# A residual block with two convolutions: image sums moved from TensorE to VectorE and ScalarE, warm-up matmuls, and the first tile's chain put ahead

## The chip, the cores and the metric

The kernel runs on one core of one Trainium2 chip, in one launch. The metric is the device time of that launch in microseconds, taken as the median of several executions. A shorter time is better.

The core has five engines that run their own instruction streams in order and wait for each other through semaphores: TensorE (PE, matrix products into the accumulator memory PSUM), VectorE (DVE), ScalarE (ACT), GpSimd (POOL) and SyncE (SP), which here issues the hardware DMAs. POOL issues the DMAs that add into their target.

## The reference, cut to what matters

Two images (B = 2) of 512 channels and 64x64 pixels go through group norm, SiLU and a 3x3 convolution, twice; an embedding is added between, and the input at the end.

```python
B, C, HW, E = 2, 512, 64, 1152
def reference(x, t_emb, g1, be1, w1, w_emb, g2, be2, w2):
    G, eps = 4, 1e-5
    def gn(z, gamma, beta):
        zr = z.reshape(B, G, (C // G) * H * W)
        mu = zr.mean(-1).reshape(B, G, 1)
        var = ((zr - mu) ** 2).mean(-1).reshape(B, G, 1)
        ...
        return zn * gamma.reshape(1, C, 1, 1) + beta.reshape(1, C, 1, 1)
    def conv3(z, w):
        taps = [jnp.einsum("bchw,oc->bohw", zp[:, :, i:i+H, j:j+W], w[:, :, i, j]) for i in range(3) for j in range(3)]
        ...
    h = conv3(_silu(gn(x, g1, be1)), w1)
    emb = _silu(t_emb) @ w_emb
    h = h + emb.reshape(B, C, 1, 1)
    h = conv3(_silu(gn(h, g2, be2)), w2)
    return x + h
```

A group of the norm is 128 channels, so it is one tile of 128 partitions: each tile needs the mean and the mean square of 128 x 4096 elements before its SiLU can start. All arrays are bf16.

## The kernel before, in words

**Tiles and chunks.** Channels are cut into four tiles `ct` of 128 partitions. The work is cut into eight chunks `c`: layer, image, half of the image's rows. Chunks 0 and 1 are image 1 in the first convolution, 2 and 3 image 2 in the first, 4 to 7 the same in the second. A chunk is four units `k`, one for each tile of output channels. The convolution is computed in a transformed form: six row points `s` = 0 to 5 (`rows_a`, `rows_b` make them on DVE out of the SiLU's output), and, from chunk 1 on, for some of the points a second transform along the columns. A unit is a sequence of matmul groups named by what they compute: `p` (three taps, moving operand of 512 columns), `B` and `A` (nested, 256 columns each). ACT copies each finished PSUM bank out (`evac_...`), DVE combines the points into the output rows.

**Order.** Nothing runs in the order in which it is written. `Plan.op` notes each operation with its engine, an estimated cost and the regions it reads and writes; `Plan.solve` schedules all of them by a list scheduler with priorities from the end backwards, and `emit` writes the instructions by their planned start. So each engine's queue is the planner's order. Main matmuls (`chain=True`) keep the order in which they were written; the others (statistics, norms, embedding) are put between them. Two numbers steer that: `slack`, a time in us by which the planner keeps such a PE operation after its inputs, and `boost`, which lets one be picked earlier.

**The opening.** For each of the four tiles of image 1 the first half (`XB0`, 34 rows of 65) and the second half (`XB1`, 32 rows) are loaded by SP, and `stats0(ct)` forms the sums:

- `ones(...)`: eight matmuls of 260 columns with a matrix of ones (`ones_bf`) for each half, which add over channels; one ACT instruction then sums the 260 columns (the mean);
- `gram(...)`: seventeen matmuls of the first half with itself (`128x128` and one `32x32`), whose diagonal a DVE instruction at L1081 takes out (mean square of the first half);
- an ACT `Square` with accumulation over 2080 elements for the mean square of the second half.

`gn_chain` then adds over partitions (small f32 matmuls with `ones_neg`), and through a few DVE instructions of one column and one power on POOL (L453) gives the scale and shift of the tile's SiLU (`silu`, ACT, 2112 elements). `rows_a` makes points 4 and 5 (one `TENSOR_SCALAR` of 2145 and three `TENSOR_TENSOR` of 1040 elements on DVE), and the 18 matmuls of these points for three output tiles follow ("o" below: 18 for each `ct`, 72 in all).

**Image 2.** `stats1(ct)` does the same for image 2, while chunk 0 computes: per tile four loads of 1040 columns into three rotating buffers, four `ones` matmuls and one ACT `Square` with accumulation for each piece, and one ACT sum of 260 columns at the end. That is 64 matmuls and 16 squares. Chunk 2 needs the result.

**Lines.** All planned matmuls stand at L381, ACT's at L353, DVE's two-operand ones at L330 and its scalings at L334, DMAs at L366.

Of the kernel before, what the change touches and what calls it, by code (L numbers as in the profile page):

```python
# [10 lines left out]
ACT = mybir.ActivationFunctionType  # L11
ALU = mybir.AluOpType
# [13 lines left out]
class Plan:  # L26
# [7 lines left out]
    def __init__(self):  # L34
        self.ops = []
        self.spaces = {}
        self.chain = None

    def _space(self, name, size):
        if name not in self.spaces:  # L40
# [6 lines left out]
    def op(self, eng, cost, fn, r=(), w=(), name="", chain=False, lat=None, slack=0.0, after=None, sw=False, boost=0.0):  # L47
        o = Op()
        o.i, o.eng, o.cost, o.fn, o.name = len(self.ops), eng, cost, fn, name
        o.lat = self.LAT[eng] if lat is None else lat  # L50
        o.slack = slack
        o.sw = sw
        o.boost = boost
        deps = set()
        for sp, idx in r:
            deps.update(np.unique(self.spaces[sp][0][idx]).tolist())
        for sp, idx in w:
            lw, rd, mask = self.spaces[sp]
# [119 lines left out]
def _idx(off, dims):  # L178
# [27 lines left out]
    's': ((A_, A_, A_), (D_, D_, D_), (D_, A_, A_), (D_, D_, D_), (A_, A_, A_), (A_, A_, D_), (A_, A_, A_), (D_, A_, D_)),  # L206
    'oacc': (1, 1),
    'np': 1,
    'pre': 13,
    'wpe': (1, 0, 0, 0),  # L210
    'vacc': (0, 1, 1, 1, 1, 1, 1, 0),
# [4 lines left out]
def kernel(  # L216
# [97 lines left out]
    def Fc(n):  # L314
        c = fcur[0]
        fcur[0] += n
        assert fcur[0] <= NF
        return c
# [4 lines left out]
    def T(ap, key):  # L323
        return R(ap, K(key), 1)
# [58 lines left out]


    make_identity(nc, ident[:])
    nc.vector.memset(ones_neg[:], -1.0 / P)
    nc.vector.memset(ones_bf[:], 1.0)
    cneg = T(ones_neg[:], "cneg")
    cone = T(ones_bf[:], "cone")
    cid = T(ident[:], "cid")  # L390
    gp, tp = T(gparm[:], "gparm"), T(tparm[:], "tparm")
    GB = Fc(4 * CT)
    EMB = Fc(CT * BB)
    SC = Fc(2 * BB * CT)
# [32 lines left out]
    def small(fn, r, w, name, cost=0.125):  # L427
        pl.op("DVE", cost, fn, regs(*r), regs(*w), name)

    def gn_chain(layer, b, ct, mes, name, SB=7, slack=2.5, n=1):  # L430

        V = nc.vector
        ps = Ps(SB, 0, [[1, 2 * n]])
# [612 lines left out]
    memz("gpsimd", A(AB[0], [[1, RW]]), "az")  # L1046
    memz("gpsimd", A(AB[1], [[1, RW]]), "az")

    def stats0(ct):
        nm = f"st0{ct}"  # L1050
        me = Fc(2)
        mg = Fc(1)
        bk = 6 + (ct % 2)
        jk = YS[1] + (ct % 2) * 1040
        G0 = 260
        b_ = psum[:]

        def ones(base, first):
            mm([(Ps(bk, 0, [[1, 260]]), cone, A(base + i * 260, [[1, 260]], BF16), first and i == 0, False)
                for i in range(8)], nm, chain=False, slack=0.0, warm=cold)  # L1060

        def gram(base, last):
            lst = []
            for i in range(17):
                n = 128 if i < 16 else 32
                blk = A(base + i * 128, [[1, n]], BF16)
                q_ = psum[0:n]
                lst.append((R(bass.AP(q_.tensor, q_.offset + bk * 512 + G0, [list(q_.ap[0]), [1, n]]),
                              ("P", np.array([bk])), n), blk, blk, False, i == 16))
            mm(lst, nm, chain=False, slack=0.0, warm=cold)  # L1070

        cold = 1.7 if ct == 0 else 1.0
        ones(XB0[ct] + RW, True)
        gram(XB0[ct] + RW, False)
        cold = 1.0
        ones(XB1[ct], False)
        x1 = A(XB1[ct], [[1, YF]], BF16)
        act(A8(jk, YF), x1, ACT.Square, scale=float(HW) ** -0.5, acc=F(me + 1), name=nm)
        g = Ps(bk, G0, [[1, 128]])
        j2 = A(MB + 1024 + (ct % 2) * 512, [[1, 128]], BF16)  # L1080
        pl.op("DVE", 0.3, lambda: nc.vector.scalar_tensor_tensor(  # L1081
            out=j2.ap, in0=g.ap, scalar=1.0 / HW, in1=ident[:], op0=ALU.mult, op1=ALU.mult, accum_out=F(mg).ap),
            regs(g), regs(j2, F(mg)), nm)
        junk = A(MB + (ct % 2) * 512, [[1, 260]], BF16)
        act(junk, Ps(bk, 0, [[1, 260]]), ACT.Identity, scale=1.0 / (P * HW), acc=F(me), name=nm)
        gn_chain(0, 0, ct, [(me, 0, 2), (mg, 1, 1)], nm, SB=bk, slack=0.0)

    IDS = {}
    for i, v in enumerate((-1.0, 2.0, -2.0, 4.0)):
# [6 lines left out]
    def pe_w1(ct):  # L1096

        nm = f"w1_0{ct}"
        d = A(RAW[ct % 2] + 1152, [[1, 384]], BF16)
        dma(d.ap, w1[0][:, 3072 + ct * 384:3072 + (ct + 1) * 384], [], [d], P * 768, nm)  # L1100
        load_ur_ct(0, ct)
        w0 = UREG[0] + 7168 + ct * 768
        lst = []
        for s, (c0, c2, c1) in enumerate(((1.0, 1.0, -1.0), (1.0, 4.0, -2.0), (1.0, 1.0, 1.0), (1.0, 4.0, 2.0))):
            for i, (cf, src) in enumerate(((c0, w0), (c2, w0 + 384), (c1, RAW[ct % 2] + 1152))):
                lst.append((Ps(s, 0, [[1, 384]]), IDS[cf], A(src, [[1, 384]], BF16), i == 0, i == 2))
        mm(lst, nm, chain=False, slack=0.0)
        act(A(UREG[0] + ct * 1792, [[128, 4], [512, 3], [1, 128]]), Ps(0, 0, [[512, 4], [128, 3], [1, 128]]), ACT.Copy, name=nm)

    for ct in range(CT):  # L1110
        if CFG["wpe"][ct]:
            pe_w1(ct)
    for ct in range(CT):
        d = A(XB0[ct], [[1, AF]], BF16)
        dma(d.ap, x[0, ct, 0], [], [d], P * AF * 2, f"x0{ct}", lat=3.1)
        d = A(XB1[ct], [[1, YF]], BF16)
# [4 lines left out]
        rows_a(0, ct, WB[ct % 3], CFG["k0"][ct], True)  # L1121
        for j in range(3):
# [13 lines left out]
    def stats1(ct):  # L1136
        nm = f"st1{ct}"
        me, mq = ME1 + ct, ME1 + CT + ct
        bk = 6 + ct % 2
        part = Fc(4)  # L1140
        for i in range(4):
# [4 lines left out]
            mm([(Ps(bk, 0, [[1, 260]]), cone, A(pb + 260 * q, [[1, 260]], BF16),  # L1146
                 i == 0 and q == 0, i == 3 and q == 3) for q in range(4)], nm, chain=False, boost=15.0)
            act(A8(VB[0] + 3 * VP + 3120 + i % 2 * 520, 1040), d, ACT.Square, scale=float(HW) ** -0.5, acc=F(part + i), name=nm)
        act(A(VB[0] + 3 * VP + 3120, [[1, 260]], BF16), Ps(bk, 0, [[1, 260]]), ACT.Identity, scale=1.0 / (P * HW), acc=F(me), name=nm)
        pl.op("DVE", 0.1, lambda: nc.vector.reduce_sum(out=F(mq).ap, in_=F(part, 4).ap, axis=AX.X),  # L1150
              regs(F(part, 4)), regs(F(mq)), nm)
        if ct == CT - 1:
            later.append(lambda: gn_chain(0, 1, 0, [(ME1, 0, 2 * CT)], "st1", n=CT))

    def emb():
        nm = "emb"
        at = [VB[0] + i // 2 * VP + 3120 + i % 2 * 512 for i in range(8)] + [JNK]
        for i in range(0, ET, 2):
# [143 lines left out]
```

## Time and profile before

| | |
|---|---|
| median of 5 runs | 468.43 us (466.42 to 469.41) |
| the profiled execution | 468.97 us |
| its span, first to last instruction | 467.2 us |
| PE, DVE, ACT busy | 452.0, 418.6, 373.1 us |
| POOL busy | 84.2 us |
| granted TensorE clock, mean | 0.998 |
| HBM read, written | 62.25, 31.32 MB |
| `ones` matmuls (128x260) | 128, busy 18.5 us |
| `gram` matmuls (128x128) | 64, busy 5.3 us |
| ACT `Square` of image 2 (128x1040) | 16, mean 1076 ns |

The profiled execution lasts 1.8 us longer than its span; it lies 0.5 us above the median. "Busy" of PE counts a matmul from its start to its modelled end, and the ends of one overlap the start of the next; the distance from one start to the next is the time that a matmul costs a full PE. ACT instructions with accumulation are followed by a short `ACTIVATION_READ_ACCUMULATOR`, most of which overlaps.

### The profile page before, as it was taken

How to read it: one execution, taken by the hardware profiler on the slowest of the kernel's cores; microseconds unless marked ns; L12 is line 12 of the kernel's file. 1: busy time of each engine (PE TensorE's matmuls, PEld its weight loads, DVE VectorE, ACT ScalarE, POOL GpSimd, SP SyncE). 2: the span in 40 equal slices, each digit the busy share in tenths (PEclk: the TensorE clock that was granted, in tenths of full speed). 3: DMA queues.
4: the chain of work that ended last, by engine and by line, in shares of the span. 5: the costliest groups of instructions: out<-in, count | busy, mean ns of one | idle time of the engine just before them, and what ended most of it. 6: DMA issues, size and time to landing. Idle time of an engine off the chain costs nothing.

```text
span 467.2 us, 8376 instructions
## 1 busy us (share of the span) xinstructions
PE 452.0 (97%) x2968; PEld 286.5 (61%) x2968; DVE 418.6 (90%) x807; ACT 373.1 (80%) x588; POOL 84.2 (18%) x110
## 2 busy tenths in 40 slices
PE   6989999999999999999999999999999999999994
PEld 5745554455555555455555576666677776678883
DVE  0599999998799999965998899989999799999997
ACT  5899999677989976889959869778776989567662
POOL 4010011121120121120211111232233211231210
PEclk9999999999999999999999999999999999999999
DMA  8974775499868589984898979867998696676834
GB/s 324 364 278 120 204 201 155 114 293 326 231 160 227 163 208 277 267 268 164 219 291 253 349 262 279 226 96 178 252 219 193 139 228 138 137 167 127 161 72 91
DMA packets 50138, 98.38 MB, mean 211 GB/s; under 512 B 7088, under 2 KB 22320, under 8 KB 50096
## 3 DMA queue, kind: packets, MB, share of 16 engines
q1 hardware_dynamic: 35520, 77.60, 48.6%
q0 software_dynamic: 14288, 20.24, 28.4%
q8 instruction: 23, 0.38, 0.3%
q14 instruction: 19, 0.16, 0.1%
q10 hardware_dynamic: 288, 0.01, 0.0%
HBM read 62.25 MB, written 31.32 MB: 200 GB/s over the span
## 4 chain that ended last, share of the span: by engine, by line
PE 46%; DVE 6%; DMA 3%; ACT 2%; issue 2%; DVEq 0%; SPq 0%; ACTq 0%
PE psum L381 46%; DVE ar L330 6%; ACT ar L353 2%; DMA ar<-u_scr 2%; DMA ar<-ar 1%; DVE ar L334 0%; DVEq L1297 0%; SPq L366 0%; DVE fs L1026 0%; DVE fs L1027 0%; DVEq L330 0%; DVE fs L1029 0%; DVE fs L1031 0%; DVE fs L1034 0%; DVE fs L1028 0%
## 5 line engine op out<-in xcount | busy, mean ns | idle before, releaser
L381 PE MATMUL psum<-ar 128*128 128x256 f16 (+2 forms) x2761 | 434.6, 319 | 1.5 <-DMA ar<-in_w_dram 1.4
L330 DVE TENSOR_TENSOR ar<-ar 128x1040 f16<-128x1040 f16 (+7 forms) x649 | 393.6, 665 | 28.9 <-ACT ar L353 19.9
L381 PEld LDWEIGHTS <-ar 128*128 128x128 f16 (+1 forms) x2797 | 269.7, 98 | 160.0 <-issue 2.2
L353 ACT ACTIVATE ar<-ar 128x384 bf16<-128x384 bf16 (+6 forms) x185 | 159.0, 898 | 46.2 <-DVE ar L330 22.8
L353 ACT ACTIVATE ar<-psum 128x512 f16<-128x512 f32 (+2 forms) x232 | 159.7, 715 | 29.2 <-PE psum L381 17.1
L366 POOL DMA_DIRECT2D ar<-ar x46 | 50.5, 1115 | 229.8 <-DVE ar L330 126.7
L353 ACT ACTIVATE ar<-ar,fs 128x2112 f16<-128x2112 bf16 (+1 forms) x32 | 68.9, 2157 | 7.0 <-DMA ar<-h_scr 2.6
L366 POOL DMA_DIRECT2D out_dram<-ar x15 | 18.5, 1234 | 48.8 <-DMA ar<-ar 30.2
L334 DVE TENSOR_SCALAR ar<-ar 128x512 f16<-128x512 f16 (+2 forms) x73 | 26.0, 383 | 1.0 <-ACT ar L353 1.0
L381 PE MATMUL psum<-ar,ones_bf 128*128 128x260 bf16 x128 | 18.5, 283 | 4.5 <-DMA ar<-in_x_dram 4.5
L353 ACT ACTIVATION_READ_ACCUMULATOR ar<-psum 128x1 f32 x100 | 21.7, 217 | 0.0
L381 PEld LDWEIGHTS <-ones_bf 128*128 128x128 bf16 x128 | 12.5, 101 | 9.6 <-issue 3.2
L370 POOL MEMSET ar<- 128x65 f16 (+6 forms) x30 | 6.4, 273 | 58.8 <-ACT ar L353 25.5
L453 POOL TENSOR_TENSOR fs<-fs 128x1 f32<-128x1 f32 (+1 forms) x7 | 7.2, 1025 | 32.3 <-DVE fs L451 32.3
L1081 DVE SCALAR_TENSOR_TENSOR ar<-psum,ident 128x128 bf16<-128x128 f32 x4 | 1.2, 289 | 8.3 <-PE psum L381 8.3
L353 ACT ACTIVATION_READ_ACCUMULATOR ar<-ar 128x1 f32 x36 | 7.6, 210 | 0.0
L381 PEld LDWEIGHTS psum<-fs,ones_neg 128*128 128x128 f32 x36 | 4.7, 191 | 3.5 <-ACT ar L353 3.3
L381 PE MATMUL psum<-fs,ones_neg 128*128 128x1 f32 (+3 forms) x36 | 4.6, 241 | 2.3 <-ACT ar L353 2.3
L444 DVE COPY fs<-psum 128x2 f32<-128x2 f32 (+1 forms) x7 | 1.1, 159 | 1.7 <-PE psum L381 1.7
L412 ACT ACT_TABLE_LOAD x1 | 1.3, 1283 | 1.7 <-PEq L1286 1.7
L416 DVE CAST fs<-gparm 128x16 f32<-128x16 bf16 x1 | 0.2, 174 | 2.6 <-DMA gparm<-in_params_dram 2.6
L417 ACT ACTIVATE s_sb<-tparm 128x18 bf16<-128x18 bf16 x1 | 0.2, 218 | 2.8 <-DMA tparm<-in_t_emb_dram 2.8
(40 smaller groups left out, 18.8 us busy)
## 6 DMA issues: line engine op xcount, KB each, us to landing
ar<-in_w_dram SPq DMA_DIRECT2D x32, 384.0 KB, 5.2
ar<-ar POOLq DMA_DIRECT2D x46, 260.0 KB, 4.9
ar<-in_x_dram SPq DMA_DIRECT2D x16, 552.5 KB, 4.5
h_scr<-ar SPq DMA_DIRECT2D x16, 520.0 KB, 5.1
ar<-h_scr SPq DMA_DIRECT2D x16, 520.0 KB, 4.6
out_dram<-in_x_dram SPq DMA_DIRECT2D x30, 260.0 KB, 5.2
out_dram<-ar POOLq DMA_DIRECT2D x15, 520.0 KB, 6.0
u_scr<-ar SPq DMA_DIRECT2D x16, 384.0 KB, 3.9
```

Source lines behind the costliest of these rows:

```text
L330: pl.op("DVE", 0.075 + 0.000521 * out.n, lambda: nc.vector.tensor_tensor(out=out.ap, in0=a.ap, in1=b.ap, op=op), regs(a, b), regs(out), name)
L334: pl.op("DVE", cost or 0.075 + 0.00026 * out.n, lambda: nc.vector.tensor_scalar(out=out.ap, in0=a.ap, scalar1=s, scalar2=None, op0=ALU.mul ...
L353: lambda: nc.scalar.activation(out=out.ap, in_=a.ap, func=func, scale=sc, **kw), regs(*rr), regs(*ww), name)
L366: lambda: eng.dma_start(out=out, in_=in_, **kw), regs(*r), regs(*w), name, lat=lat or (4.5 if sw else None), after=after, sw=sw)
L370: pl.op("POOL" if eng == "gpsimd" else "DVE", 0.08 + 0.0005 * out.n, lambda: e.memset(out.ap, v), (), regs(out), name)
L381: nc.tensor.matmul(out.ap, lhsT=lhsT.ap, rhs=rhs.ap, start=st, stop=sp, skip_group_check=True)
L412: nc.scalar.activation(out=fs[:, WARM:WARM + 1], in_=fs[:, WARM + 1:WARM + 2], func=ACT.Silu)
L416: nc.vector.tensor_copy(out=fs[:, GB:GB + 4 * CT], in_=gparm[:])
L417: nc.scalar.activation(out=s_sb[:], in_=tparm[:], func=ACT.Silu)
L444: pl.op("DVE", 0.16, lambda: V.tensor_copy(out=F(tot, 2 * n).ap, in_=ps.ap), regs(ps), regs(F(tot, 2 * n)), name, boost=bo)
L453: pl.op("POOL", 0.85 if n == 1 else 1.9, lambda: nc.gpsimd.tensor_tensor(out=F(rs, n).ap, in0=N.ap, in1=F(NEGH, n).ap, op=ALU.pow), regs(N ...
L1081: pl.op("DVE", 0.3, lambda: nc.vector.scalar_tensor_tensor(out=j2.ap, in0=g.ap, scalar=1.0 / HW, in1=ident[:], op0=ALU.mult, op1=ALU.mult, ...
```

## The change

1. **Image 1's sums** (`stats0`), by a table `'st0'` with a letter for each half of each tile: `D` is `bn_stats` on DVE (five pieces of 416 elements, then `bn_aggr` and two small instructions that turn mean and variance into mean and mean square); `A` is the `ones` matmuls with ACT's square; `P` is the `ones` matmuls with the gram. The table is `('DA', 'DA', 'DP', 'PP')`.
2. **Image 2's sums** (`stats1`): for each piece ACT runs a second pass, `Identity` with accumulation, in place of the four `ones` matmuls; a DVE `reduce_sum` adds the four partial sums.
3. **Warm-up**: nine matmuls of 512 columns on `ones_bf`, with no data to wait for, before all others.
4. **First tile ahead**: `push` adds to the boost of all operations of tile 0's chain (40, and 20 more for its first load).
5. **Smaller pieces**: `gram` is planned as two operations, the weights' `pe_w1` matmuls as four, the embedding's 36 as nine, the latter with `slack` 0 for 2.5.
6. **`slack` of `gn_chain`** by default 5.0 for 2.5, which concerns image 2's first norm and both norms of the second layer.

```diff
-        o.boost = boost
+        o.boost = boost + self.push
...
+    'st0': ('DA', 'DA', 'DP', 'PP'),
+    'st1': 'AAAA',
+    'warm': 9,
+    'push': (40.0, 0.0, 0.0, 0.0),
...
+    for i in range(CFG["warm"]):
+        nc.tensor.matmul(psum[:, 0:512], lhsT=ones_bf[:], rhs=wr, start=True, stop=True, skip_group_check=True)
...
-    def gn_chain(layer, b, ct, mes, name, SB=7, slack=2.5, n=1):
+    def gn_chain(layer, b, ct, mes, name, SB=7, slack=5.0, n=1):
...
+    def bn(pieces, out, scale, name):
+        mv = Fc(2)
+        V = nc.vector
+        for i, d in enumerate(pieces):
+            pl.op("DVE", 0.07 + 0.00104 * d.n, lambda d=d, i=i: V.bn_stats(out=F(BNS + 6 * i, 6).ap, in_=d.ap),
+                  regs(d), regs(F(BNS + 6 * i, 6)), name)
+        S_, M_, W_ = F(BNS, 6 * len(pieces)), F(mv), F(mv + 1)
+        small(lambda: V.bn_aggr(out=F(mv, 2).ap, in_=S_.ap), [S_], [F(mv, 2)], name, 0.15)
...
+        for h, base in enumerate((XB0[ct] + RW, XB1[ct])):
+            if how[h] == "D":
+                me = Fc(2)
+                bn([A(base + i * 416, [[1, 416]], BF16) for i in range(5)], F(me, 2), YF / HW, nm)
+                mes.append((me, 0, 2))
+                continue
+            ones(base, cold)
+            if how[h] == "P":
+                gram(base, cold, "P" not in how[h + 1:])
+            else:
+                sq = Fc(1)
+                act(A8(jk, YF), A(base, [[1, YF]], BF16), ACT.Square, scale=float(HW) ** -0.5, acc=F(sq), name=nm)
+                mes.append((sq, 1, 1))
...
-        mm(lst, nm, chain=False, slack=0.0)
+        for i in range(0, 12, 3):
+            mm(lst[i:i + 3], nm, chain=False, slack=0.0)
...
+        pl.push = CFG["push"][ct]
+        pl.push += 20.0 if ct == 0 else 0.0
...
+            if CFG["st1"][ct] == "A":
+                act(A8(VB[0] + 3 * VP + 3120 + i % 2 * 520, 1040), d, ACT.Identity, scale=1.0 / HW, acc=F(psum_ + i), name=nm)
...
-        mm(lst, nm, chain=False)
+        for i in range(0, len(lst), CT):
+            mm(lst[i:i + CT], nm, chain=False, slack=0.0)
```

Since the planner orders everything anew, the queues of all engines differ from before, also where the operations are the same.

More of the change, by code (lines that the diff above doesn't have):

```diff
@@ L37, in __init__ @@
         self.chain = None
+        self.push = 0.0
     def _space(self, name, size):
@@ L385 @@
     make_identity(nc, ident[:])
+    nc.vector.memset(ones_bf[:], 1.0)
     nc.vector.memset(ones_neg[:], -1.0 / P)
-    nc.vector.memset(ones_bf[:], 1.0)
     cneg = T(ones_neg[:], "cneg")
@@ L391 @@
     gp, tp = T(gparm[:], "gparm"), T(tparm[:], "tparm")
+    wr = ones_bf[:]
+    wr = bass.AP(wr.tensor, wr.offset, [list(wr.ap[0]), [0, 4], [1, P]])
+    for i in range(CFG["warm"]):
+        nc.tensor.matmul(psum[:, 0:512], lhsT=ones_bf[:], rhs=wr, start=True, stop=True, skip_group_check=True)
     GB = Fc(4 * CT)
@@ L1047 @@
     memz("gpsimd", A(AB[1], [[1, RW]]), "az")
+    BNS = Fc(96)
+    def bn(pieces, out, scale, name):
[6 more added lines that the diff above has]
+        small(lambda: V.bn_aggr(out=F(mv, 2).ap, in_=S_.ap), [S_], [F(mv, 2)], name, 0.15)
+        small(lambda: V.scalar_tensor_tensor(
+            out=W_.ap, in0=M_.ap, scalar=M_.ap, in1=W_.ap, op0=ALU.mult, op1=ALU.add), [M_, W_], [W_], name)
+        small(lambda: V.tensor_scalar(
+            out=out.ap, in0=F(mv, 2).ap, scalar1=scale, scalar2=None, op0=ALU.mult), [F(mv, 2)], [out], name)
     def stats0(ct):
         nm = f"st0{ct}"
-        me = Fc(2)
-        mg = Fc(1)
         bk = 6 + (ct % 2)
@@ L1055, in stats0, with ones, gram @@
         G0 = 260
-        b_ = psum[:]
-        def ones(base, first):
-            mm([(Ps(bk, 0, [[1, 260]]), cone, A(base + i * 260, [[1, 260]], BF16), first and i == 0, False)
+        how = CFG["st0"][ct]
+        begun = []
+        def ones(base, cold):
+            mm([(Ps(bk, 0, [[1, 260]]), cone, A(base + i * 260, [[1, 260]], BF16), not begun and i == 0, False)
                 for i in range(8)], nm, chain=False, slack=0.0, warm=cold)
-        def gram(base, last):
+            begun.append(0)
+        def gram(base, cold, last):
             lst = []
@@ L1068, in gram @@
                 lst.append((R(bass.AP(q_.tensor, q_.offset + bk * 512 + G0, [list(q_.ap[0]), [1, n]]),
[L1069 to L1086, printed above, removed]
+                              ("P", np.array([bk])), n), blk, blk, False, last and i == 16))
@@ new lines, in gram @@
+            mm(lst[:8], nm, chain=False, slack=0.0, warm=cold)
+            mm(lst[8:], nm, chain=False, slack=0.0, warm=cold)
+        mes = []
+        for h, base in enumerate((XB0[ct] + RW, XB1[ct])):
+            cold = 1.0
+            if how[h] == "D":
[10 more added lines that the diff above has]
+                mes.append((sq, 1, 1))
@@ new lines, in stats0 @@
+        if "P" in how:
+            mg = Fc(1)
+            g = Ps(bk, G0, [[1, 128]])
+            j2 = A(MB + 1024 + (ct % 2) * 512, [[1, 128]], BF16)
+            pl.op("DVE", 0.3, lambda: nc.vector.scalar_tensor_tensor(
+                out=j2.ap, in0=g.ap, scalar=1.0 / HW, in1=ident[:], op0=ALU.mult, op1=ALU.mult, accum_out=F(mg).ap),
+                regs(g), regs(j2, F(mg)), nm)
+            mes.append((mg, 1, 1))
+        if begun:
+            s1 = Fc(1)
+            junk = A(MB + (ct % 2) * 512, [[1, 260]], BF16)
+            act(junk, Ps(bk, 0, [[1, 260]]), ACT.Identity, scale=1.0 / (P * HW), acc=F(s1), name=nm)
+            mes.insert(0, (s1, 0, 1))
@@ L1088 @@
+        gn_chain(0, 0, ct, mes, nm, SB=bk, slack=0.0)
     IDS = {}
@@ L1113 @@
     for ct in range(CT):
+        pl.push = CFG["push"][ct]
+        pl.push += 20.0 if ct == 0 else 0.0
         d = A(XB0[ct], [[1, AF]], BF16)
         dma(d.ap, x[0, ct, 0], [], [d], P * AF * 2, f"x0{ct}", lat=3.1)
+        pl.push = CFG["push"][ct]
         d = A(XB1[ct], [[1, YF]], BF16)
@@ L1121 @@
         rows_a(0, ct, WB[ct % 3], CFG["k0"][ct], True)
+        pl.push = 0.0
         for j in range(3):
@@ L1138, in stats1 @@
         me, mq = ME1 + ct, ME1 + CT + ct
+        use_bn = CFG["st1"][ct] == "D"
         bk = 6 + ct % 2
         part = Fc(4)
+        psum_ = Fc(4)
+        pieces = []
         for i in range(4):
@@ L1145, in stats1 @@
             dma(d.ap, x[1, ct, i // 2][:, r0 * RW:(r0 + 16) * RW], [], [d], P * 2080, nm)
-            mm([(Ps(bk, 0, [[1, 260]]), cone, A(pb + 260 * q, [[1, 260]], BF16),
-                 i == 0 and q == 0, i == 3 and q == 3) for q in range(4)], nm, chain=False, boost=15.0)
-            act(A8(VB[0] + 3 * VP + 3120 + i % 2 * 520, 1040), d, ACT.Square, scale=float(HW) ** -0.5, acc=F(part + i), name=nm)
-        act(A(VB[0] + 3 * VP + 3120, [[1, 260]], BF16), Ps(bk, 0, [[1, 260]]), ACT.Identity, scale=1.0 / (P * HW), acc=F(me), name=nm)
-        pl.op("DVE", 0.1, lambda: nc.vector.reduce_sum(out=F(mq).ap, in_=F(part, 4).ap, axis=AX.X),
-              regs(F(part, 4)), regs(F(mq)), nm)
+            if use_bn:
+                pieces += [A(pb + 260 * q, [[1, 260]], BF16) for q in range(4)]
+                continue
+            if CFG["st1"][ct] == "A":
+                act(A8(VB[0] + 3 * VP + 3120 + i % 2 * 520, 1040), d, ACT.Identity, scale=1.0 / HW, acc=F(psum_ + i), name=nm)
+            else:
+              mm([(Ps(bk, 0, [[1, 260]]), cone, A(pb + 260 * q, [[1, 260]], BF16),
+                   i == 0 and q == 0, i == 3 and q == 3) for q in range(4)], nm, chain=False, boost=15.0)
+            act(A8(VB[0] + 3 * VP + 3120 + i % 2 * 520, 1040), d, ACT.Square, scale=float(HW) ** -0.5, acc=F(part + i), name=nm)
+        if use_bn:
+            bn(pieces, Fs(me, CT, 2), 2 * YF / HW, nm)
+        else:
+          if CFG["st1"][ct] == "A":
+            pl.op("DVE", 0.1, lambda: nc.vector.reduce_sum(out=F(me).ap, in_=F(psum_, 4).ap, axis=AX.X),
+                  regs(F(psum_, 4)), regs(F(me)), nm)
+          else:
+            act(A(VB[0] + 3 * VP + 3120, [[1, 260]], BF16), Ps(bk, 0, [[1, 260]]), ACT.Identity, scale=1.0 / (P * HW), acc=F(me), name=nm)
+          pl.op("DVE", 0.1, lambda: nc.vector.reduce_sum(out=F(mq).ap, in_=F(part, 4).ap, axis=AX.X),
+                regs(F(part, 4)), regs(F(mq)), nm)
         if ct == CT - 1:
```

## The prediction, made before the changed kernel ran

> **What bounds the kernel now.** First the page's busy lines and slices, then PE's waits, the windows by stage, and the timeline.
>
> ```profile
> PE 452.0 (97%) x2968; PEld 286.5 (61%) x2968; DVE 418.6 (90%) x807; ACT 373.1 (80%) x588; POOL 84.2 (18%) x110
> PE   6989999999999999999999999999999999999994
> ...
> PE psum L381 <- DMA ar<-in_x_dram: 4.5, 1, 4.5
> PE psum L381 <- ACT ar L353: 2.3, 2, 1.4
> PE psum L381 <- DMA ar<-in_w_dram: 1.4, 1, 1.4
> ...
> 20.00:40.00 20.00, 18.61 (x135) 10.34 (x133) 19.28 (x46) 20.00 (x29) 1.49 (x2) 1.00 0.72 240
> 40.00:60.00 20.00, 20.00 (x108) 10.33 (x106) 19.65 (x42) 19.77 (x50) 1.07 (x1) 1.00 0.63 177
> 60.00:80.00 20.00, 20.00 (x102) 9.74 (x101) 19.61 (x39) 19.63 (x39) 2.21 (x3) 1.00 0.63 178
> 80.00:100.00 20.00, 20.00 (x98) 9.40 (x97) 19.79 (x41) 13.09 (x31) 3.62 (x3) 1.00 0.67 180
> 100.00:130.00 30.00, 30.00 (x175) 16.86 (x173) 24.46 (x53) 25.99 (x48) 4.76 (x4) 1.00 0.91 284
> ```
>
> The waits say that PE stands four times: 4.5 us for the first load, 1.39 at 32.76, 0.88 and 1.39 for ACT. In the windows the columns after the stretch are PE, PEld, DVE, ACT, POOL: PE never rests from 34 us on, but from 20 to 80 DVE and ACT are just as full. ACT has room only after 80. So PE's work is the bound, with two others close behind.
>
> ```profile
> 4.47 1.89 PE L381 MATMUL psum<-ar,ones_bf 128*128 128x260 bf16 x8 [4.47 <-DMA ar<-in_x_dram]
> 16.12 2.14 ACT L353 ACTIVATE ar<-ar,fs 128x2112 f16<-128x2112 bf16 x1
> 33.67 1.07 ACT L353 ACTIVATE ar<-ar 128x1040 fp8e4<-128x1040 bf16 x1
> 34.73 1.06 ACT L353 ACTIVATE ar<-ar 128x1040 fp8e4<-128x1040 bf16 x1
> ...
> 32.76 3.50 PE L381 MATMUL psum<-ar 128*128 128x512 f16 x15 [1.39 <-DMA ar<-in_w_dram]
> ...
> 49.45 0.61 PE L381 MATMUL psum<-ar,ones_bf 128*128 128x260 bf16 x4
> 49.90 0.83 PE L381 MATMUL psum<-ar 128*128 128x512 f16 x3
> 50.57 0.61 PE L381 MATMUL psum<-ar,ones_bf 128*128 128x260 bf16 x4
> ...
> 193.26 0.61 PE L381 MATMUL psum<-fs,ones_neg 128*128 128x8 f32 x4 [0.88 <-ACT ar L353]
> 304.77 0.61 PE L381 MATMUL psum<-fs,ones_neg 128*128 128x8 f32 x4 [1.39 <-ACT ar L353]
> ```
>
> Starts give prices: four `ones` cost 49.90-49.45 = 0.45 us, 0.1125 each; three main matmuls 0.67, 0.222 each, so PE is packed. The wait at 32.76 is put down to a load, but pairing the queue's order with the trace shows that the third tile's last row product on DVE ended 0.05 us before: the opening is paced by the tiles' statistics, SiLUs and rows.
>
> The same pairing gives PE's lead over its inputs: between 40 and 150 us every matmul started at least 3.5 us after the DVE result and 2.2 us after the ACT result that it uses. That is the room that a faster PE can use up. It is 3.5 to 4.6 us behind DVE in chunk 0, and 5.8 at the start of chunk 2 (155.7 us).
>
> **The Trainium skill.** "Perfetto Trace Analysis", Identifying the Most-Contended Engine, warns that matmul busy time is no measure of PE; hence the start distances above. "TensorE: Matmul & The Clock Gate", What's actually happening, puts a cold PE at 1.2 of 2.4 GHz, until some 3.4 us of activity: agreed, the first eight `ones` took 6.16-4.47 = 1.69 us to the next group's start, 0.211 each against 0.1125. "VectorE: DVE Perf Modes", the section on the trn2 errata, gives `58 + FD/Accel` cycles at 0.96 GHz; for 416 elements at one a cycle my estimate for a `bn_stats` is 0.49 us. No such instruction is in this trace.
>
> **PE, removed and added.** `ones` fall from 128 to 40: 24 of image 1, 64 of image 2. 88 x 0.1125 = 9.9 us. One `gram` less, 17 matmuls, 1.17 us (in the timeline one starts at 9.96, the group behind it at 11.13). The norms' sums take three more small f32 matmuls, about 0.6. Sum: 10.5 us less PE work. The nine warm-ups run cold (9 x 0.427 = 3.8 us, twice 512/2.4) from about 1.0 to 4.9, while the first operand lands at about 5.3: hidden, and they remove the cold start (8 x 0.1 + 17 x 0.05 = 1.6 us). Without that cover they would cost at most 0.5.
>
> **The opening.** What counts is when the third tile's matmuls start (32.76 before), since from there PE is fed. DVE's queue after: five `bn_stats` from 4.9 (after the 4.6 cast of the parameters) to 7.4; ACT's square and sum of the first tile end at 8.7, its small matmuls and copy at 9.7. Then the queue puts the five `bn_stats` of the second tile between the chain's small instructions, so the first SiLU starts not at 11 but at about 12.8 (16.12 before). Its rows end at 18 (first "o" matmul, 21.71 before). But the next SiLU stands in ACT's queue behind the weights' copy (1.36 us) and six scalings (0.41 each), and that of the first tile of chunk 1 is put ahead of the third tile's. Adding the start distances of before along DVE's queue: 16.6 us of work between the first rows' first instruction (14.8 to 15.3) and the third tile's last row, with about 0.5 of waits for PE's small matmuls: 32.5 us. So 0.3 us gained, and the 3.3 us of image 1's matmuls and the warm clock go into PE's idle time in front of it. Loads don't decide: 10.1 MB stand before the last embedding load, at some 400 GB/s in the first 20 us they end at 28 to 29, and PE asks at 29 to 30. Cost from both sides for this step: with `bn_stats` at 0.43 (no fixed cost) 31.5, with twice the price 37 to 38.
>
> **Image 2's sums.** From there 64 `ones` x 0.1125 = 7.2 us are gone, all between 36 and 71 us. ACT gets 16 passes of 1040 elements for four sums of 260 (0.36 each) and two squares of 2080 (1.97 each) of image 1: the nearest row, the square of the same size, starts every 1.06 us; 16 x 1.06 - 1.4 - 3.9 = 11.6 us more. From 20 to 80 ACT has no room for that; its queue after shows what gives way: image 2's squares and sums stretch to behind the last unit of chunk 0, and the squares of `h` and the weights of the second layer, which nobody needs before 190 us, go behind. Evacuations keep their places. By the sums, PSUM banks come free 0.5 to 3 us before PE needs them from 75 to 105 us. DVE's row and weight products for units 1 to 3 lie 3 to 4 us ahead of PE. Nothing there is late by my sums, but nothing has more than 4 us.
>
> The late place is the start of chunk 2. ACT's queue from the first SiLU to chunk 2's last scaling holds 134.2 us of start distances; before, ACT took 2.7% more than that sum between its first SiLU and its end of the fourth SiLU of chunk 1 (56.8 for 55.3). 12.8 + 134.2 x 1.027 = 150.6, two short DVE instructions after it partly beside other work. PE would reach that matmul at 32.5 + 116.2 of its own work = 148.7. I take 1.8 us of waiting, between 0 (ACT at the bare sum) and 5 (6% over it).
>
> **The norms' slack.** The two waits of 0.88 and 1.39 us came because PE met the small matmul 4.7 us after the last matmul of its bank, while ACT's evacuation of that bank was just ending. With `slack` 5.0 they stand 6.4 and 5.9 us after it. 2.3 us gone, if ACT isn't later; behind the waiting matmul the whole unit stands. Nothing is added: the SiLUs of the next chunk were 3.5 us or more ahead. The tail after the last matmul (7 us) has the same queues as before.
>
> **Sum.** 0.3 + 7.2 + 2.3 - 1.8 = 8.0 us. Span 467.2 - 8.0 = 459.2; with the 1.8 us around it 461.0 for a profiled execution like that of before (468.97); taken from the median, 460.4. I round to 460.5.
>
> **Rivals.**
> A: ACT is the bound in chunks 0 to 2. For: it is full from 20 to 80, and gets 11.6 us more. Against: 13 us of what it did before 130 us can wait (four squares of 1.97, seven pairs of scalings of 0.41). Four more us of waiting at chunk 2: 464.4.
> B: PE is fed everywhere, no wait at chunk 2 and an opening 1 us earlier: 468.4 - 10.8 = 457.6. Against: DVE 98% full from 20 to 100.
> C: `bn_stats` costs twice (0.98). Ten stand before the first SiLU and the others before the third tile's rows, 15 x 0.49 less 2 of idle: third tile 5 us later, gain 8 - 5.3 = 2.7, further late rows 1 us: 466.8, no change that can be told.
> D, slower: image 2's pieces hold ACT. Three buffers; a load is issued only when the piece two passes before is done, by SP, whose queue in order also waits for DVE and ACT elsewhere; ACT waits in order with the evacuations behind it, and PE stands on full PSUM. In before SP spent 20.0 us waiting for PE in the first 60 us, but ACT only 2.4 us for `in_x_dram` in the whole span. It decides from 0.65 us of waiting for each of 16 pieces (10.4 us: the gain and 0.5%); at 1 us each, 468.4 + 8 = 476.
>
> **How the numbers follow.** Forecast 0.50 (458.5 to 463), A 0.20, B 0.10, C 0.08, D 0.12. Faster by over 0.5% (2.3 us, about what a measurement here can tell from no change): 0.80; within 0.08; slower 0.12. The range from 456.5 to 467 leaves out D and a little of B.
>
> **What would show it.** Right: PE's `ones` 40; the first SiLU at 12 to 14 us; third tile's "o" matmuls at 31.5 to 34; no PE wait for ACT at the two norms; some PE wait near 149 us; ACT full to 150. Wrong: `bn_stats` starting more than 0.6 us apart, PE waits for ACT between 45 and 105 us, ACT waits for `in_x_dram` above 5 us, or PE's clock below 1.00 in the first 35 us.

## The result and the profile after

| | before | after |
|---|---|---|
| median of all runs | 468.21 us (48 runs) | 472.73 us (469.25 to 478.41, 27 runs) |
| after to before | | 1.0092, interval 1.0074 to 1.0111 |
| profiled execution, its span | 468.97, 467.2 us | 473.33, 471.5 us |

The changed kernel is 0.9% slower, 4.3 us, where 1.7% faster was forecast. The ratio leaves out three executions of the changed kernel that took over 476.2 us, 1.5% more than its fastest; with them the medians differ by 4.5 us. TensorE (PE) has less to do, and stands more. The page of the kernel after, its busy lines and slices:

```profile
PE 447.7 (95%) x2878; PEld 278.9 (59%) x2878; DVE 425.4 (90%) x831; ACT 383.3 (81%) x608; POOL 84.8 (18%) x110
...
PE   7979999999989999999999989999999699999993
...
PEclk9999999999999999999999999999999899999998
```

PE's line has a 6, and its clock an 8, in the slice that starts at 365 us (the 32nd of 11.8 us). The waits of PE in the kernel after say for whom; the five largest (us in total, times, longest):

```profile
PE psum L386 <- ACT ar L358: 9.6, 6, 3.9
PE psum L386 <- DVE ar L335: 2.5, 2, 1.8
PE psum L386 <- DMA ar<-in_x_dram: 2.3, 3, 1.1
PE psum L400 <- DVE ones_bf L391: 1.1, 1, 1.1
PE psum L386 <- DVE fs L453: 0.8, 1, 0.8
```

Before, PE waited 2.3 us for ACT in two places; now 9.6 in six. Three timelines of the kernel after, DVE, ACT and PE, show the first 310 us (start, us, instructions, idle before and what ended it):

```profile
5.28 2.05 DVE L1064 BATCH_NORM_STATS2 fs<-ar 128x6 f32<-128x416 bf16 x4
...
13.26 2.15 ACT L358 ACTIVATE ar<-ar,fs 128x2112 f16<-128x2112 bf16 x1 [2.20 <-DVE fs L466]
...
1.06 3.94 PE L400 MATMUL psum<-ones_bf 128*128 128x512 bf16 x9 [1.06 <-DVE ones_bf L391]
...
33.00 1.27 PE L386 MATMUL psum<-ar 128*128 128x512 f16 x5 [1.76 <-DVE ar L335]
...
140.69 9.61 PE L386 MATMUL psum<-ar 128*128 128x256 f16 x50 [1.28 <-ACT ar L358]
...
189.76 0.50 PE L386 MATMUL psum<-fs,ones_neg 128*128 128x8 f32 x4
```

The opening and the norm at 190 us are as forecast. The wait of 1.28 us at 140.69 is not the one forecast for the start of chunk 2. When the planner's order of each engine is laid beside its trace, the wait lies in the last unit of chunk 1: PE needs a PSUM bank that ACT evacuates from 139.97 to 140.55, behind a SiLU of chunk 2 that waited 0.62 us for its load of `x`. The matmul of chunk 2 that started at 155.7 before starts at 150.58, without a wait.

The same timeline of PE from 261 to 380 us, in the second layer:

```profile
275.15 12.49 PE L386 MATMUL psum<-ar 128*128 128x256 f16 x88 [2.25 <-ACT ar L358]
288.38 14.90 PE L386 MATMUL psum<-ar 128*128 128x256 f16 x107 [0.74 <-ACT ar L358]
303.12 0.50 PE L386 MATMUL psum<-fs,ones_neg 128*128 128x8 f32 x4
...
308.27 27.48 PE L386 MATMUL psum<-ar 128*128 128x512 f16 x188 [0.81 <-DVE fs L453]
336.33 32.79 PE L386 MATMUL psum<-ar 128*128 128x256 f16 x236 [0.57 <-ACT ar L358]
373.02 7.22 PE L386 MATMUL psum<-ar 128*128 128x256 f16 x37 [3.90 <-ACT ar L358]
```

Here the gain is lost. By the same pairing, matmul by matmul, PE is 6.8 us ahead of the kernel before at 72 us (a time of the kernel before), 6.3 at the end of chunk 3 (268 us), 3.3 at the start of chunk 5, and 3.2 us behind in the first unit of chunk 6.

**The stall at 373 us** can be followed back. ACT's timeline after:

```profile
361.45 0.60 ACT L358 ACTIVATE ar<-psum 128x512 f16<-128x512 f32 x1 [1.64 <-DMA ar<-ar]
363.68 1.68 ACT L358 ACTIVATE ar<-ar 128x512 f16<-128x512 f16 x3 [1.63 <-DVE ar L335]
365.26 0.58 ACT L358 ACTIVATE ar<-psum 128x512 f16<-128x512 f32 x1
369.92 2.15 ACT L358 ACTIVATE ar<-ar,fs 128x2112 f16<-128x2112 f16 x1 [4.08 <-DMA ar<-h_scr]
371.97 1.92 ACT L358 ACTIVATE ar<-psum 128x1024 f16<-128x1024 f32 x2
```

The instruction at 369.92 is a SiLU of chunk 7, whose rows PE uses only from about 421 us on; it stands 4.08 us for its load from `h_scr`, and the evacuations of PSUM at 371.97 stand behind it. PE needs that PSUM. The load's own line in the list of transfers of the kernel after:

```profile
ar<-h_scr SPq DMA_DIRECT2D x1, 520.0 KB, 6.8
```

And in the kernel before:

```profile
ar<-h_scr SPq DMA_DIRECT2D x1, 520.0 KB, 3.4
```

The last number is from issue to landing. The Trainium skill, "SBUF — State Buffer", The DMA setup-cost knee, fits about 2 us plus the bytes at 436 GB/s, my estimate 3.2 us for 532,480 bytes. The load of before agrees; after's took twice that, issued beside an output store of 520 KB and two weight loads of 384 KB. It was also issued 3.9 us later (363.04 for 359.13), because VectorE (DVE) reached the last reader of its buffer 3.9 us later (row product begun at 362.28 for 358.37). By my estimate either one put right would nearly have spared the stall: issued at 363.04 and landing after 3.4 us, the load holds the SiLU 0.6 us; issued at 359.13 and landing after 6.8 us, 0.1. Over the whole span ACT waits 12.3 us for `h_scr`, 2.6 before.

And the idle time is not all of it. Windows of PE in the kernel after (busy, granted clock, DMA share, GB/s):

```profile
366.00:373.00 7.00, 3.12 (x17) 1.00 0.85 247
373.00:376.00 3.00, 2.98 (x16) 0.57 0.00 0
376.00:379.00 3.00, 3.00 (x14) 0.86 0.07 9
```

After 3.9 us of idleness the clock was 0.57 over the next 3 us: from this unit's first to its third set of products PE took 6.08 us (373.02 to 379.10), 4.42 before. The stall cost 3.9 + 1.7 us.

### The profile page after: what moved, and what is told of

Its sections match the earlier page's. It is cut to its first block, busy times and chain, and to the rows that moved or that the text cites. A ratio compares the mean times of both kernels' runs of the same rounds, so it can differ in the third digit from the quotient of the medians.

```text
span 471.5 us, 8217 instructions
## 1 busy us (share of the span) xinstructions
PE 447.7 (95%) x2878; PEld 278.9 (59%) x2878; DVE 425.4 (90%) x831; ACT 383.3 (81%) x608; POOL 84.8 (18%) x110
## 5 line engine op out<-in xcount | busy, mean ns | idle before, releaser
L335 DVE TENSOR_TENSOR ar<-ar 128x1024 f16<-128x1024 f16 (+6 forms) x649 | 392.5, 665 | 27.7 <-ACT ar L358 16.0
L358 ACT ACTIVATE ar<-ar 128x384 bf16<-128x384 bf16 (+6 forms) x199 | 169.8, 899 | 39.4 <-DVE ar L335 23.7
L358 ACT ACTIVATE ar<-psum 128x512 f16<-128x512 f32 (+3 forms) x228 | 156.3, 718 | 19.5 <-DVE ar L335 9.7
L358 ACT ACTIVATE ar<-ar,fs 128x2112 f16<-128x2112 bf16 (+1 forms) x32 | 68.7, 2150 | 17.2 <-DMA ar<-h_scr 12.3
L358 ACT ACTIVATION_READ_ACCUMULATOR ar<-psum 128x1 f32 x96 | 20.5, 214 | 0.0
L358 ACT ACTIVATION_READ_ACCUMULATOR ar<-ar 128x1 f32 x50 | 10.4, 208 | 0.0
L1064 DVE BATCH_NORM_STATS2 fs<-ar 128x6 f32<-128x416 bf16 x15 | 8.1, 581 | 0.0
L386 PE MATMUL psum<-ar,ones_bf 128*128 128x260 bf16 x40 | 5.3, 274 | 2.3 <-DMA ar<-in_x_dram 2.3
L386 PEld LDWEIGHTS <-ones_bf 128*128 128x128 bf16 x40 | 3.8, 99 | 3.9 <-issue 2.6
L400 PE MATMUL psum<-ones_bf 128*128 128x512 bf16 x9 | 3.9, 622 | 1.1 <-DVE ones_bf L391 1.1
L400 PEld LDWEIGHTS <-ones_bf 128*128 128x128 bf16 x9 | 1.2, 143 | 3.0 <-issue 1.9
```

The lines of the kernel that those rows point to most:

```text
L335: pl.op("DVE", 0.075 + 0.000521 * out.n, lambda: nc.vector.tensor_tensor(out=out.ap, in0=a.ap, in1=b.ap, op=op), regs(a, b), regs(out), name)
L358: lambda: nc.scalar.activation(out=out.ap, in_=a.ap, func=func, scale=sc, **kw), regs(*rr), regs(*ww), name)
L386: nc.tensor.matmul(out.ap, lhsT=lhsT.ap, rhs=rhs.ap, start=st, stop=sp, skip_group_check=True)
L400: nc.tensor.matmul(psum[:, 0:512], lhsT=ones_bf[:], rhs=wr, start=True, stop=True, skip_group_check=True)
L1064: pl.op("DVE", 0.07 + 0.00104 * d.n, lambda d=d, i=i: V.bn_stats(out=F(BNS + 6 * i, 6).ap, in_=d.ap), regs(d), regs(F(BNS + 6 * i, 6)), name)
```

## The experiments

Three theories: LEAD, that ACT, DVE and the loads set the pace of the second layer, so that PE's lead is lost there; DEBT, that the moved sums make DVE and ACT late; ORDER, that the new queues of the second layer are at fault. Since the queues are the planner's, there are three kinds of experiment: work left out with the queues kept; one place in a queue changed; and the same work planned anew. Of the edits only the core is shown.

**1. Less PE work in the queues of before** (`b_few_ones`).

```diff
         for o in sorted(self.ops, key=lambda o: (o.start, o.i)):
+            n = seen[o.name, o.eng] = seen.get((o.name, o.eng), -1) + 1
+            if o.eng == "PE" and o.name in ("st10", "st11", "st12", "st13") and n < 3:
+                continue
             o.fn()
```

> The kernel before with every queue as it was, but 48 of the 64 sum matmuls of image 2 left out (the sums of three of four pieces are missing from the mean): PE has 48 x 0.1125 = 5.4 us less to do, no other engine less or more. If PE paces the kernel to its end: 462.8 (5.4 less than 468.2). Theory LEAD (the second layer is paced by DVE, ACT and loads, so that a lead of PE is lost there): 467 to 469. Theories DEBT (the moved sums make DVE and ACT late) and ORDER (the new plan's queues in the second layer are at fault): like PE-paced, 462 to 464, since neither load nor order is changed here.

467.40 us, ratio 0.9991 (0.9971 to 1.0011): 5.4 us of matmuls gone, nothing gained. In its timeline of PE:

```profile
68.27 0.61 PE L385 MATMUL psum<-ar,ones_bf 128*128 128x260 bf16 x4 [1.57 <-DMA ar<-in_x_dram]
...
192.29 0.61 PE L385 MATMUL psum<-fs,ones_neg 128*128 128x8 f32 x4 [1.80 <-ACT ar L357]
```

PE was 3.8 us ahead at 66 us and lost 1.6 to a load that the remaining sums need. At the norm it waited 1.80 us (0.88 before), and behind that wait the granted clock was 0.79 over the 8 us from 192 to 200, which is 1.7 us more; by 197 us PE was 0.7 behind. So the work taken from PE came back as waits for a load and for ACT, and as lost clock. The time is the one that LEAD expected, but the place is the first layer, not the second, so LEAD is not tested there.

**2. The moved work left out, in the queues of after** (`a_no_ident`, `a_few_bn`).

```diff
                 act(..., ACT.Identity, scale=1.0 / HW, acc=F(psum_ + i), name=nm)
+                pl.ops[-1].fn = lambda: None
...
             pl.op("DVE", ..., lambda d=d, i=i: V.bn_stats(...), ...)
+            if i:
+                pl.ops[-1].fn = lambda: None
```

> The changed kernel with every queue as it is, but the 16 Identity passes of image 2's sums left out (image 2's mean stays zero): ACT has 16.8 us less to do before 100 us. DEBT, if ACT's part of it counts: 465 to 468. ORDER: 472 to 473, as the changed kernel. LEAD: 470 to 473, the lead is lost all the same.

> The changed kernel with every queue as it is, but 12 of the 15 bn_stats left out (the first halves' sums come from one piece of five): DVE has 6.5 us less to do before 19 us and the first SiLU comes some 4 us earlier. DEBT, if DVE's part counts: 466 to 469. ORDER: 471 to 473. LEAD: 471 to 473.

473.18 us, ratio 1.0094 (1.0056 to 1.0131), and 472.78 us, ratio 1.0102 (1.0067 to 1.0136). Neither moves the time. The load that the change puts on ACT and DVE is not what makes the kernel slower, as long as the queues stay.

**3. The second layer placed as in before** (`a_l2_before`): its operations sorted by the start times that the planner gave them in the kernel before, less 6.75 us.

```diff
+            key.append(old[k][j] - SHIFT if k in old else o.start)
```

> The changed kernel, but all operations of the second layer (chunks 4 to 7, the second norm, their loads and stores) are put into the queues by the planned times of the kernel before, less 6.75 us; the first layer and the preparation of the second weights stay as in the changed kernel. ORDER: the loss of 10 us after 273 us goes, 461 to 464. DEBT: 470 to 473, since the late products stay late. LEAD: 467 to 470, as before.

484.18 us, ratio 1.0361 (1.0311 to 1.0410). Its timeline of PE:

```profile
239.44 4.58 PE L404 MATMUL psum<-ar 128*128 128x512 f16 x28 [2.78 <-ACT ar L376]
254.16 8.02 PE L404 MATMUL psum<-ar 128*128 128x512 f16 x34 [10.14 <-ACT ar L376]
```

The two halves don't fit at the seam: two stalls in chunk 3 cost 13 us. As a test of after's second layer it failed. But no instruction was added or removed, so places in the queues alone are worth over 10 us.

**4. One instruction moved** (`o_silu71`): the SiLU that stood at 369.92, behind three evacuations.

```diff
+MOVES = (("ACT", "silu71", 0, "u53m1", 0),)
...
+            key[at[eng, name][n]] = key[at[eng, late][m]] + 0.001
```

> After's queues with one instruction moved: on ScalarE the SiLU of chunk 7's second tile goes behind the evacuations u53b, u53m0 and u53m1 that stood behind it while it waited 4.08 us for its load (until 369.92 us). ORDER (a queue place in the second layer makes the loss): the 3.9 us idle stretch of TensorE at 373 us goes, and with it the slices at a lower TensorE clock behind it (about 1.5 us): 472.7 - 5.4 = 467.3 us, with the earlier stalls at 275 and 288 us left as they are. DEBT (the moved sums make VectorE and ScalarE late whatever the order): the wait comes back one instruction on, at chunk 7's first rows, and the time stays at 471 to 473 us.

468.74 us, ratio 0.9996 (0.9971 to 1.0021), against 1.0092 of after: about 0.96%, 4.5 us, of the 5.4 expected by ORDER. Its timeline of PE has no wait at 373 us:

```profile
277.71 10.74 PE L402 MATMUL psum<-ar 128*128 128x256 f16 x72 [2.25 <-ACT ar L374]
...
339.13 41.13 PE L402 MATMUL psum<-ar 128*128 128x256 f16 x300 [0.29 <-ACT ar L374]
```

The stall of chunk 4 stays, as it should.

**5. The same instructions in queues planned anew** (`r_lat28`, `s_lat32`, `s_lat36`, `s_lat45`: another latency of loads in the plan; `r_gn25`: the slack of the norms back at 2.5).

```diff
-    LAT = {"PE": 0.12, "DVE": 0.12, "ACT": 0.15, "POOL": 0.15, "DMA": 2.4}
+    LAT = {"PE": 0.12, "DVE": 0.12, "ACT": 0.15, "POOL": 0.15, "DMA": 2.8}
```

> After's instructions, all of them, in queues planned anew: the planner is told 2.8 us instead of 2.4 us for the fixed part of a load from HBM (the trace of after shows 4.6 us from issue to landing for the tile loads where the plan has 3.8). ORDER: the lead of TensorE at 273 us (5.8 us) is kept to the end by queues that happen to be better, and the time is 462 to 467 us. DEBT: same work, same time, 471 to 474 us.

> After with one part of the change undone: the slack of the norms' chains is 2.5 us again. No work changes, but the planner writes other queues. ORDER: another draw of queues, the time moves by some us in either direction (463 to 476 us), mainly through waits in the second layer. DEBT: 471 to 474 us; at most the 0.9 to 1.4 us of the norms' waits come back on top.

`r_lat28` took 459.88 us in four executions, ratio 0.9826 (0.9788 to 0.9865); `r_gn25` 467.96, ratio 1.0005 (0.9980 to 1.0030). The first beats both kernels, with the instructions of after, and by more than ORDER expected (462 to 467). The largest of its waits of PE:

```profile
PE psum L386 <- DMA ar<-in_x_dram: 2.3, 3, 0.8
PE psum L386 <- DVE ar L335: 2.1, 4, 1.0
PE psum L386 <- ACT ar L358: 2.1, 3, 1.0
```

Windows of the kernel after in the second half (PE, PEld, DVE, ACT, POOL busy):

```profile
200.00:272.00 72.00, 71.81 (x410) 39.85 (x408) 59.42 (x107) 59.33 (x102) 8.85 (x16) 1.00 0.89 269
272.00:340.00 68.00, 63.63 (x454) 44.30 (x453) 63.86 (x107) 53.54 (x61) 16.81 (x19) 1.00 0.86 224
340.00:400.00 60.00, 56.10 (x387) 38.38 (x386) 53.29 (x80) 44.24 (x49) 13.27 (x15) 0.97 0.75 169
```

And of `r_lat28`:

```profile
200.00:272.00 72.00, 71.92 (x418) 40.71 (x416) 63.95 (x117) 60.08 (x101) 9.96 (x17) 1.00 0.91 281
272.00:340.00 68.00, 67.04 (x477) 46.53 (x476) 65.38 (x105) 55.84 (x64) 17.33 (x21) 1.00 0.93 218
340.00:400.00 60.00, 60.00 (x429) 41.81 (x428) 57.13 (x86) 47.02 (x51) 13.42 (x14) 1.00 0.79 174
```

And the first window of the kernel before:

```profile
200.00:272.00 72.00, 72.00 (x413) 40.17 (x411) 58.84 (x108) 58.14 (x100) 10.50 (x17) 1.00 0.81 244
```

Look at the first rows: PE is full in all three, so nothing seems wrong in after; but DVE did 59.4 us of work there and 63.95 in `r_lat28`, while the kernel before has 58.84. PE in after came 6 us earlier to engines that hadn't moved. I read the 4.5 us that DVE did less as a debt that PE pays in the next two rows (63.6 and 56.1 for 67.0 and 60.0). That is a reading and not shown: the 3.9 us of the last row are the stall that one move in ACT's queue took away.

Was 459.9 us the rule or luck? Three more draws (each new plan of the same work is a draw of queues):

> After's instructions, planned with 3.2 us for the fixed part of a load. If after's queues were the odd ones: 459 to 463 us, with under 5 us of TensorE's waits. If 459.9 us was a lucky draw: anywhere from 462 to 474 us, with several us of waits of TensorE for ScalarE or VectorE in the second layer.

> The same with 3.6 us. If after's queues were the odd ones: 459 to 463 us. If 459.9 us was a lucky draw: 462 to 474 us.

> The same with 4.5 us, nearly what the trace shows from issue to landing. If a planner that expects loads late makes queues that keep TensorE's lead: 458 to 463 us. If later loads in the plan only cost room elsewhere: 464 us or more.

466.49, 466.91 and 466.31 us, ratios 0.9953 (0.9929 to 0.9977), 0.9962 (0.9935 to 0.9989) and 0.9961 (0.9946 to 0.9975). So it was luck, by the expectation's own measure; a planner that expects loads later isn't better for it. In `s_lat32` the waits lie at 306, 319 and 427 us (1.48, 1.44, 1.20).

**6. The kernel before in other queues** (`b_lat28`, `sb_lat36`; the edit of 5).

> The kernel before with its queues planned anew by the same edit as r_lat28 (2.8 us instead of 2.4 us for the fixed part of a load), no part of the change in it. If the new draw of queues alone brings what r_lat28 has (the change itself is worth nothing), it falls to 460 to 462 us. If the change's work is what r_lat28 gains and only its queues in after spoilt it, the kernel before stays at 466 to 469 us, since its TensorE has only some 6 us of waits to lose at all.

> The kernel before, planned with 3.6 us. Its TensorE waited 6 us in all, so a better draw has little to win: 464 to 469 us; a bad draw can lose as after did: up to 475 us. Below 463 us would say that the change's work is worth less than the 8.9 us between r_lat28 and b_lat28.

468.88 us, ratio 1.0002 (0.9984 to 1.0020), and 469.28 us, ratio 1.0010 (0.9989 to 1.0031). Three draws of before lie within 0.1% (ratios 1 to 1.0010), six of after within 2.7% (0.9826 to 1.0092).

**7. Parts taken back, with a new plan** (`r_st1_back` from after; the other three from `r_lat28`).

```diff
-    'st1': 'AAAA',
+    'st1': 'PPPP',
...
-    'st0': ('DA', 'DA', 'DP', 'PP'),
+    'st0': ('PA', 'PA', 'PA', 'PA'),
...
-    'warm': 9,
+    'warm': 0,
```

> After with the sums of image 2 back on TensorE (64 matmuls with ones), no Identity passes on ScalarE, everything planned anew. If the image-2 part is what makes the change slower (DEBT, by its loads and its 16 ScalarE passes), the time falls below before's: 468 - 2 to 3 us from the first tiles' and opening's part. If that part gave the 7.2 us that the prediction gave it and the loss lies elsewhere, the time rises by about 5 to 7 us to 478 us. ORDER alone: anything from 466 to 478 us, with the loss at other places than 275 and 373 us.

> r_lat28 with the sums of image 2 back on TensorE (64 matmuls with ones at 0.1125 us) and no Identity passes. The prediction's price of this part is 7.2 us: 459.9 + 7.2 = 467.1 us. If the part is worth less than its matmuls because ScalarE is short, 461 to 464 us. A bad draw of queues in the second layer would add waits of TensorE there, to be read off its waits: 468 to 474 us.

> r_lat28 with all four tiles of image 1 back on the sums by ones and gram matmuls: no bn_stats, no gram saved. The prediction's price of this part is the 24 ones, the 17 gram matmuls and the small ones of the end of the opening: 24 x 0.1125 + 1.2 + the opening's effect, 3 to 4 us: 463 to 464 us. If bn_stats only moves work to a VectorE that has none to spare: 459 to 460 us.

> r_lat28 with the nine warm-up matmuls left out, the same queues otherwise. If the warm-ups buy nothing, since the first tile's own matmuls warm TensorE up behind waits for loads: 459.9 us, within 0.5. If they buy a warm start: some 0.5 to 1.5 us more, seen in the first twenty microseconds of TensorE alone.

468.19 us, ratio 1.0021 (1.0002 to 1.0040); 471.95, ratio 1.0076 (1.0052 to 1.0100); 466.34, ratio 0.9951 (0.9932 to 0.9971); 461.01, ratio 0.9840 (0.9812 to 0.9868). Against the expectations: 471.95 lies in the range of a bad draw and not at 467.1, 466.34 lies above the 463 to 464, and 461.01 is 1.1 us above 459.88, where a warm start was to bring 0.5 to 1.5. At their ends these runs mix the part's price with a draw of queues: by the ratios, image 2's sums cost 3.3 us less on PE than on ACT in one plan, 12 us more in the other. The table tells the two apart. It has the lead of PE on the kernel before in the profiled executions, in us, at five landmarks of PE's work (named by the time at which before passes them), and at the end by the spans:

| | 72 | 268 | 322 | 376 | 413 | end |
|---|---|---|---|---|---|---|
| after | 6.8 | 6.3 | 3.3 | -3.2 | -3.2 | -4.3 |
| `o_silu71` | 4.7 | 4.8 | 0.3 | -0.3 | -0.3 | -1.9 |
| `r_gn25` | 3.8 | 4.9 | 1.5 | 1.5 | 1.5 | 1.2 |
| `s_lat32` | 4.0 | 5.0 | 5.3 | 3.4 | 3.4 | 1.8 |
| `s_lat36` | 5.5 | 6.3 | 5.7 | 4.8 | 3.7 | 0.9 |
| `s_lat45` | 2.1 | 2.9 | 4.4 | 4.4 | 4.4 | 2.0 |
| `r_lat28` | 7.8 | 7.6 | 8.6 | 8.0 | 8.0 | 7.3 |
| `r28_no_warm` | 6.8 | 7.8 | 8.4 | 8.1 | 8.1 | 8.0 |
| `r28_st0_back` | 4.4 | 4.3 | 6.2 | 6.2 | 4.2 | 1.9 |
| `r28_st1_back` | -0.1 | 0.6 | 0.7 | 0.7 | 0.7 | -2.0 |
| `r_st1_back` | 0.4 | 1.1 | 3.1 | 3.1 | 3.1 | 2.0 |
| `b_few_ones` | 2.6 | -0.7 | 1.3 | 1.3 | 1.3 | 1.3 |
| `b_lat28` | 0.6 | 1.3 | 0.4 | 0.4 | 0.4 | 0.4 |

`o_silu71` has after's queues up to 365 us and yet 2.1 us less at 72. Most of that is the clock: over the 8 us from 32 to 40 us it is 0.79 in this trace, which is 1.7 us, and 1.00 in after's. It is 0.79 in `r_gn25`, `s_lat32` and `s_lat45` too. So a difference of two single traces under about 2 us says nothing by itself. In the rows compared next the clock is 1.00 there. At 72 us image 2's sums are worth 7.9 us in one plan (7.8 + 0.1) and 6.4 in the other (6.8 - 0.4); image 1's 3.4 (7.8 - 4.4); the warm-ups 1.0 (7.8 - 6.8). The kernel without them has the queues of `r_lat28`; its first "o" matmul starts at 19.54 for 18.48, and the two are level again from 139 us on, where `r_lat28` waits 0.97 us for ACT. From 268 us on, where all these kernels have the same instructions, the rows go their own ways: from -10.6 us in after to +2.0 in `b_few_ones`.

The six draws of after also show how far the reading of DVE's debt goes. By 272 us DVE had worked 239.8 us in after, 240.6 in `r_gn25`, 242.5, 243.7 and 243.9 in `s_lat32`, `s_lat36` and `s_lat45`, 244.6 in `r_lat28`; from 268 to 376 us PE's lead changed by -9.5, -3.4, -1.6, -1.5, +1.5 and +0.4 us. By and large the draws in which DVE had done more by then lost less (1.7 us of the 3.4 in `r_gn25` are clock, at 277 us). Six traces that agree are not yet a cause.

## Why the prediction was wrong, by its steps

- **PE's work, opening, image 2's sums: right.** Warm-ups from 1.06 to 5.00; first SiLU at 13.26 (forecast 12.8); first "o" matmul at 18.7 (18); third tile at 33.00 (32.5), so -0.2 us instead of +0.3; image 2's sums 6.4 to 7.9 us (7.2).
- **The wait at the start of chunk 2: the size right, the place and the reason not.** The forecast 1.8 us were for ACT's last scaling of chunk 2's rows and the DVE instructions behind it; no matmul of that chunk's start waits. The 1.28 us came in the last unit of chunk 1, for an evacuation behind a SiLU that waited for its load; the prediction had that as rival D, for other loads, and had counted on evacuations that "keep their places". With the first norm's wait gone, the forecast lead at 268 us is 0.3 + 7.2 - 1.8 + 0.9 = 6.6 us; the measured 6.3 agrees in part by luck.
- **The norms: right.** Neither small matmul waits, as the lines at 189.76 and 303.12 show; at the second one PE gained 2.0 us for the forecast 1.4, and gave back 0.81 five us later to DVE's copy of that bank.
- **What failed is "Nothing is added", and with it the "Sum".** Both carry the lead of the first layer unchanged to the end. The term left out, chunks 4 to 7, was sized at nothing and measured about -12.6 us: 6.3 at 268 us, +2.0 at the second norm, -4.3 at the end. Waits account for 9.1 of it (2.25 + 0.74 + 0.81 + 0.57 + 3.90, and 0.85 at 432.81), the clock after the longest for 1.7; some 1.8 us are not accounted for one by one. The prediction had read PE's lead over its inputs from 40 to 150 us only. The same pairing of the trace of before gives, in the second layer, 0.3 us over ACT in chunk 4's first unit, 0.05 in its second, 1.4 at the end of chunk 5, 0.5 in chunk 7: PE and ACT already went hand in hand there, and 6 us of lead had nowhere to go unless ACT and DVE came earlier too. They could only do so by the queues; the prediction took them to keep pace, and never looked.
- **The rivals: the side right, the mechanism not.** D had ACT held by image 2's pieces; in the kernel after ACT waits 0.6 us for `in_x_dram`, once, ahead of the wait of 1.28 us. A's further 4 us at chunk 2 and C's dear `bn_stats` (0.49 us apart, as estimated) didn't come. The case that came, a load in the second layer holding ACT with evacuations behind it, was D's mechanism in another place, at 4.1 us for one load.
- **All the marks that were to show it right or wrong lie before 305 us**, and all but one came out right: the wait forecast near 149 us came at 140.69. None looked at the part of the span where the queues were new and the work old.

What is shown: the loss lies behind 268 us; it isn't the engine time of the moved sums; one place in ACT's queue makes 4.5 us of it; and with the same instructions other queues give 459.9 to 468 us. LEAD and ORDER are both part of it: PE's lead over ACT in the second layer was short before, and whether a new lead lasts depends on the queues. DEBT, in the sense of too much work on ACT and DVE, fell. What stays open is what makes `r_lat28`'s queues better. One difference is seen: the preparation of the second layer's weights, which in after runs from about 180 to 220 us, comes mostly 4 to 14 us earlier there on DVE and ACT. That this is the cause wasn't tried.

## What to carry to other kernels

Work taken from the engine that bounds a kernel is paid out at the end only if the engines that feed it are ahead there too: read its lead over each of them in every stage, down to the last, before adding up gains of the first. Where a planner or scheduler writes the queues, any edit draws new ones. Judge it over several draws: here the change gains about 8 us at its best, about 2 us in three draws and nothing in a fourth, and the draw that came with it lost 4.3. In an in-order queue, an instruction that waits for a load goes behind those that free PSUM. And read the granted clock behind each wait of PE: a wait can cost more than its length.

## What the runs showed of the hardware

- After 3.9 us without matmuls the granted clock was 0.57 over the next 3 us, and the 6 us from there cost 1.7 us more than at full clock. The Trainium skill, "TensorE: Matmul & The Clock Gate", What's actually happening, has half clock after at least one idle window of about 3.4 us; this stall agrees.
- Shorter waits had the same effect, and there the traces differ from that section. Before the third tile PE stood 1.89 us in `o_silu71`, 2.69 in `r_gn25`, 1.58 in `s_lat45` and 1.47 in `s_lat32`, and the clock over 32 to 40 us is 0.79 in each (0.21 x 8 = 1.7 us); after 1.76 us in the kernel after it is 1.00. In `r_gn25` 2.06 us up to 275.83 were enough too: 0.66 and 0.50 in the next two windows of 2 us from 276 on. What decides in which trace the clock falls isn't shown.
- `bn_stats` on 416 bf16 elements starts every 0.49 us back to back (four in 2.05, the last of them 0.58 long: 1.47 / 3); the `bn_aggr` behind five of them takes 0.29.
- The nine warm-up matmuls brought 1.0 us up to the first wait for ACT and nothing that can be told at the end: 461.01 us without them and 459.88 with them, four executions each, their intervals nearly the same.
